# A planned attention and Fourier kernel: three quarters of the allowance for late transfers, a transfer rate three per cent higher

## The chip, the core and the metric

The kernel runs on one core of a Trainium2 chip. The metric is the device time of one execution in microseconds. Three runs of the kernel before took 2845.42, 2845.14 and 2843.12 us, so the median is 2845.14 us. The engines are PE (matrix products), ACT (exponentials and copies), DVE and POOL (elementwise work and reductions) and SP, which here only issues DMA transfers. Each engine works through its own list of instructions in order.

## The reference

Two independent blocks are computed in float32 and set side by side: a 32-head attention over 2048 positions of width 1024, and the real part of a two-dimensional Fourier transform, written as matrix products.

```python
B, S, D = 1, 2048, 1024          # H = 32 heads of Dh = 32
qkv = (x @ wqkv).reshape(B, S, 3, H, Dh)            # -> q, k, v by head
scores = einsum("bhqd,bhkd->bhqk", q, k) * Dh ** -0.5
a = einsum("bhqk,bhkd->bhqd", softmax(scores), v)   # -> (B, S, D) @ wo
u = einsum("bsd,ed->bse", xB, dft_hid_re);  w = einsum("bsd,ed->bse", xB, dft_hid_im)
b = einsum("ts,bse->bte", dft_seq_re, u) - einsum("ts,bse->bte", dft_seq_im, w)
out = concatenate([a @ wo, b], axis=-1)             # (1, 2048, 2048)
```

## The kernel before

The dense products (the projections to q, k and v, the Fourier products and the output projection) are done by a fast matrix scheme with seven products in place of eight, for the Fourier part nested twice. Each float32 operand is split into a rounded high part and the remaining low part, and each product is made of three matmuls: high by high, low by high and high by low. One such matmul is a **fill** (line 436, tiles `slot` and `hl`): 128 rows by 512 columns. The program has 6528 of them. Their operands come from DRAM: SP loads a block (`raw`, `g`, `er`, `c`, `slot`), DVE or POOL adds or subtracts two blocks (lines 501, 1312, 1354), ACT or DVE makes the high part (lines 521 and 523), POOL or DVE makes the low part (line 526). Partial sums are taken from PSUM by DVE, and stored to DRAM and read again where they don't fit in SBUF.

Attention runs head by head beside the fills. For each head PE makes scores twice: as `psS` (line 1875, letter S in the code), of which DVE takes the row maximum (line 1881) and ACT the exponential with its sum (line 1884), to get the softmax's scale; and as `psT` (line 1997, letter T), transposed and with the maximum already subtracted, of which ACT makes the exponential into `pt` (line 2001). The products of `pt` with the values (line 2016, letter V) come in runs of 20 or 24 instructions. `psS` and `psT` have two buffers each, so PE can be only two score blocks ahead of ACT.

Nothing here is ordered by the chip alone. A planner in the kernel (class `Plan`) lists every operation with its engine, a cost, what it must wait for and a rank, plays the program through in time on the host, and writes each engine's instructions down in the order in which they begin in that play. On the chip only this order is left: each instruction still waits for its true inputs. An engine whose next instruction waits for a late input stands still, with all that is listed behind it.

The planner's picture of a transfer has four numbers. Transfers follow one another at `KB_US` KiB per microsecond; a transfer lands `LANDING` (1.6 us) after its bytes; up to eight are under way; and a consumer may be placed only after the landing plus `SLACK`, an allowance by the pair of engines. `Plan.after` adds it:

```python
return d.end + (self.LAT_PE if e == "PE" else self.LAT) + self.SLACK.get((e, o.engine), 0.0)
```

The pairs are SP to POOL, SP to DVE and SP to PE; there is no pair SP to ACT. The main loop gives PE its next instruction: an attention matmul when its inputs and buffers are ready and attention is behind its share, otherwise the next fill of a fixed list, and attention again where that fill's inputs are not ready.

Of the kernel before, what the change touches and what calls it, by code (L numbers as in the profile page):

```python
# [62 lines left out]
class Plan:  # L63
# [5 lines left out]
    LAT_PE = 0.2  # L69
    OVERLAP = {"ACT": 0.13, "DVE": 0.08, "POOL": 0.08}  # L70

    SLACK = {("SP", "POOL"): 2.0, ("SP", "DVE"): 2.0, ("SP", "PE"): 2.0, ("POOL", "DVE"): 0.7}
    KB_US = 335.0
    WIDE = 0.875
    LANDING = 1.6
    QUEUE = 1.0
# [45 lines left out]
    def after(self, d, e, o):  # L122
        return d.end + (self.LAT_PE if e == "PE" else self.LAT) + self.SLACK.get((e, o.engine), 0.0)

# [7 lines left out]
    def start(self, o, e=None):  # L132
# [11 lines left out]
        if o.kb:  # L144
            for _ in range(o.lanes):
                t = max(self.free[e], self.lane[0])
                self.dma = max(self.dma, t) + o.kb / o.lanes / self.KB_US * (self.WIDE if o.wide else 1.0)
                o.end = self.dma + self.LANDING
# [2039 lines left out]
```

## Time and profile before

| what | value |
|---|---|
| median of three runs | 2845.14 us |
| profiled execution, its own time | 2845.67 us |
| its span, first to last instruction | 2843.9 us |
| outside the span | 1.8 us |
| PE busy | 2800.9 us, 98% |
| ACT busy, DVE busy | 2368.0 us and 2362.7 us, 83% each |
| POOL busy | 1212.9 us, 43% |
| moved by DMA | 768.18 MB, mean 270 GB/s |

A row of waits names the waiting instruction, an arrow, who ended the wait, and then the sum in microseconds, how many there were and the longest. A row of windows gives a stretch of the span, its length, each engine's busy time in it with the number of its instructions, the granted clock, the share of time in which the DMA engines were busy, and the bytes per second. A row of the timeline gives the start, the length and the instruction, with the idle time ahead of it in square brackets. The length of a matmul is that of the pipeline; the pace is read from one start to the next.

### The profile page before, as it was taken

To read this page: it belongs to the slowest core of one execution; us is meant where nothing else is said; L and a number is where in the kernel's file an instruction comes from. 1 tells how busy PE (TensorE), PEld (TensorE's weight loads), DVE (VectorE), ACT (ScalarE), POOL (GpSimd) and SP (SyncE) were. 2 spreads that over 40 slices of the span, in tenths; PEclk is the share of its full clock that TensorE was granted. 3 is DMA by queue.
4 is the path that set the end of the run, shared out by engine and by line. 5 is a ranking of instruction groups with operands and counts; after the bars stand their busy time and mean duration, and the time that the engine had idled before them with its cause. 6 is when DMAs were issued, how large, how long until landed. Compare 5 with 4: busy or idle time off the path is not lost.

```text
span 2843.9 us, 47011 instructions
## 1 busy us (share of the span) xinstructions
PE 2800.9 (98%) x14728; PEld 2104.3 (74%) x14728; DVE 2362.7 (83%) x3265; ACT 2368.0 (83%) x4509; POOL 1212.9 (43%) x961
## 2 busy tenths in 40 slices
PE   9999999999999999999999999999999999999999
PEld 8787776777777777777676777777677777777777
DVE  7668888778888888799888999888888898888844
ACT  5348898878988998889898898899998898898861
POOL 1235544232334443356454445666764542243300
PEclk9999999999999999999999999999999999999999
DMA  9989979699799999877899766889957675677648
GB/s 348 342 299 331 319 254 307 211 334 327 263 318 322 335 310 334 264 237 246 294 337 337 248 208 217 296 288 280 298 171 222 219 223 172 212 236 245 188 132 280
DMA packets 485845, 768.18 MB, mean 270 GB/s; under 512 B 120383, under 2 KB 153407, under 8 KB 485471
## 3 DMA queue, kind: packets, MB, share of 16 engines
q1 hardware_dynamic: 485452, 765.04, 81.4%
q8 instruction: 119, 1.95, 0.3%
q14 instruction: 130, 1.06, 0.1%
q10 hardware_dynamic: 144, 0.13, 0.0%
HBM read 511.74 MB, written 253.25 MB: 269 GB/s over the span
## 4 chain that ended last, share of the span: by engine, by line
PE 83%; DMA 7%; ACT 6%; DVE 2%; issue 1%; SPq 1%; POOL 0%; DVEq 0%; POOLq 0%; ACTq 0%
PE pd L436 37%; PE pd L2016 14%; PE psT L1997 14%; PE psS L1875 13%; PE psT L436 4%; ACT psS L1884 3%; ACT pt L2001 2%; DVE negm L1881 1%; DMA slot<-in_ct 1%; DMA tb_d<-slot 1%; DMA si_d<-slot 1%; DMA qs<-qk_d 1%; DMA ks<-qk_d 1%; DMA m_d<-lt 1%; DMA qs<-m_d 0%
## 5 line engine op out<-in xcount | busy, mean ns | idle before, releaser
L436 PE MATMUL pd<-slot,hl 128*128 128x512 f32 x5112 | 1417.1, 379 | 4.4 <-ACT hl L521 2.3
L2001 ACT ACTIVATE pt<-psT 128x512 f32<-128x512 f32 x2048 | 1209.4, 683 | 226.7 <-PE psT L1997 225.1
L1881 DVE TENSOR_REDUCE negm<-psS 128x1 f32<-128x1024 f32 x1024 | 1240.4, 1219 | 149.8 <-PE psS L1875 134.1
L1884 ACT ACTIVATE psS<-psS,negm 128x1024 f32<-128x1024 f32 x1024 | 1215.5, 1187 | 56.4 <-DVE negm L1881 55.4
L436 PEld LDWEIGHTS pd<-slot,hl 128*128 128x128 f32 x5112 | 965.7, 189 | 137.8 <-ACT hl L521 2.7
L1997 PE MATMUL psT<-qs,ks 128*128 128x512 f32 x2048 | 784.4, 386 | 2.8 <-DMA qs<-m_d 1.3
L1997 PEld LDWEIGHTS psT<-qs,ks 128*128 128x128 f32 x2048 | 383.7, 188 | 155.6 <-issue 46.9
L1875 PE MATMUL psS<-ks,qs 128*128 128x512 f32 x1552 | 458.2, 381 | 12.0 <-ACT psS L1884 11.8
L2016 PE MATMUL pd<-pt,vt 128*32 128x512 f32 x4096 | 463.7, 599 | 2.9 <-DVE c L695 1.8
L526 POOL TENSOR_TENSOR slot<-raw,slot 128x512 fp32r<-128x512 f32 x159 | 202.0, 1277 | 326.9 <-ACT slot L521 104.8
L1875 PEld LDWEIGHTS psS<-ks,qs 128*128 128x128 f32 x1552 | 286.2, 189 | 67.9 <-ACT psS L1884 24.0
L2016 PEld LDWEIGHTS pd<-pt,vt 128*32 128x32 f32 x4096 | 124.2, 110 | 286.3 <-issue 268.4
L526 POOL TENSOR_TENSOR slot<-slot,slot 128x512 fp32r<-128x512 f32 x193 | 244.6, 1279 | 203.6 <-DVE slot L523 44.5
L1884 ACT ACTIVATION_READ_ACCUMULATOR psS<-psS,negm 128x1 f32 x1024 | 314.5, 307 | 0.0
L526 POOL TENSOR_TENSOR hl<-raw,hl 128x512 fp32r<-128x512 f32 x127 | 161.8, 1276 | 228.4 <-DVE hl L523 66.2
L501 POOL TENSOR_TENSOR raw<-raw,g 128x512 f32<-128x512 f32 x126 | 161.9, 1290 | 218.8 <-DVE hl L523 28.4
L436 PE MATMUL pd<-slot,slot 128*128 128x512 f32 x780 | 201.6, 379 | 0.4 <-DVE e L745 0.4
L436 PEld LDWEIGHTS pd<-slot,slot 128*128 128x128 f32 x780 | 147.3, 189 | 21.4 <-DVE e L745 0.9
L1875 PE MATMUL psS<-ks,qx 128*128 128x512 f32 x496 | 148.2, 389 | 10.9 <-ACT psS L1884 8.9
L1875 PEld LDWEIGHTS psS<-ks,qx 128*128 128x128 f32 x496 | 90.5, 190 | 40.0 <-ACT psS L1884 15.0
L501 DVE TENSOR_TENSOR raw<-raw,g 128x512 f32<-128x512 f32 x134 | 100.0, 755 | 15.6 <-DMA g<-g_d 4.4
L2029 DVE TENSOR_TENSOR ot<-ot,pd 128x512 f32<-128x512 f32 x64 | 43.9, 685 | 70.9 <-PE pd L2016 70.1
(140 smaller groups left out, 2121.5 us busy)
## 6 DMA issues: line engine op xcount, KB each, us to landing
hl<-ha_d SPq DMA_DIRECT2D x134, 512.0 KB
slot<-in_ct SPq DMA_DIRECT2D x144, 256.0 KB
qk_d<-e SPq DMA_DIRECT2D x52, 512.0 KB
qs<-qk_d SPq DMA_DIRECT2D x128, 192.0 KB
ks<-qk_d SPq DMA_DIRECT2D x128, 192.0 KB
raw<-g_d SPq DMA_DIRECT2D x96, 256.0 KB
ha_d<-hl SPq DMA_DIRECT2D x42, 512.0 KB
raw<-in_ct SPq DMA_DIRECT2D x80, 256.0 KB
```

What stands on the lines that cost most here:

```text
L436: nc.tensor.matmul(box["ps"], a[1]((a[0].hi, a[0].lo)[u]()), turns((b[0].hi, b[0].lo)[v]()), start=k == 0, stop=k == n - 1)
L501: (nc.gpsimd if e == "POOL" else nc.vector).tensor_tensor(out=dest(), in0=dest() if a is None else a.get(), in1=other["q"] if "q" in other ...
L526: (nc.gpsimd if e == "POOL" else nc.vector).tensor_tensor(out=lo(), in0=raw(), in1=f(hi()), op=ALU.subtract)
L1875: nc.tensor.matmul(p[:, i * NB : i * NB + NB], (QX[0] if own else QS[h % 2])[:, qt * P : qt * P + P], turns(KS[h % 2][:, c * 1024 + i * NB ...
L1881: nc.vector.tensor_reduce(out=ST["negm"][:, c, qt : qt + 1], in_=box["p"], axis=AX.X, op=ALU.max, negate=True)
L1884: nc.scalar.activation(box["p"], box["p"], AF.Exp, bias=ST["negm"][:, c, qt : qt + 1], accum_out=ST["sums"][:, c, qt : qt + 1])
L1997: nc.tensor.matmul(box["p"], KS[h % 2][:, t * P : t * P + P], turns(QS[h % 2][:, j * NB : j * NB + NB]), start=True, stop=True)
L2001: nc.scalar.activation(box["t"], box["p"], AF.Exp)
L2016: nc.tensor.matmul(po["p"][j * DH : j * DH + DH, :], VT[h][:, k, :], box["t"], start=(k == t0), stop=(k == t), tile_position=(0, j * DH),)
L2029: nc.vector.tensor_tensor(out=as_two(po["o"]), in0=as_two(po["o"]), in1=order_of(po["p"]), op=ALU.add)
```

## The change

Three entries of `SLACK` go from 2.0 to 1.5 us, and `KB_US` goes from 335 to 345 KiB per microsecond. No operation is added or removed; the planner plays the same work with transfers that take less time and consumers that may follow 0.5 us earlier.

```diff
-    SLACK = {("SP", "POOL"): 2.0, ("SP", "DVE"): 2.0, ("SP", "PE"): 2.0, ("POOL", "DVE"): 0.7}
-    KB_US = 335.0
+    SLACK = {("SP", "POOL"): 1.5, ("SP", "DVE"): 1.5, ("SP", "PE"): 1.5, ("POOL", "DVE"): 0.7}
+    KB_US = 345.0
```

The order of all engines changes almost from the start. The number of matmuls of each kind stays the same. Nineteen elementwise instructions leave DVE: ten more stand on POOL (959 for 949), nine more on ACT. Counted over PE's order, 135 of the score pairs `psS` had no fill between them and the next pair, and now 138; with two fills or fewer it was 196, and now 193. When the last head's attention ends, 264 fills were left, and now 290.

PE, where the third head ends, around the 1512th fill, before. An S row with x2 is one score block; `qx` is a copy of a part of q, `pd` the PSUM tile that fills and V share:

```order
L436 MATMUL pd<-slot_5302,slot_5505 128x512 x3
L436 MATMUL pd<-slot_5347,slot_5615 128x512 x3
L1875 MATMUL psS<-ks_710,qx 128x512 x2
L1997 MATMUL psT<-qs_2707,ks_2708 128x512 x2
L1875 MATMUL psS<-ks_710,qx 128x512 x2
L1997 MATMUL psT<-qs_2707,ks_2708 128x512
L1875 MATMUL psS<-ks_710,qx 128x512 x4
L2016 MATMUL pd<-pt,vt 32x512 x24
L1875 MATMUL psS<-ks_710,qs_709 128x512 x4
L436 MATMUL pd<-slot_5183,slot_5478 128x512 x2
```

The same fills now:

```order
L436 MATMUL pd<-slot_5300,slot_5626 128x512 x3
L436 MATMUL pd<-slot_5305,slot_5639 128x512
L1875 MATMUL psS<-ks_710,qs_709 128x512 x2
L1997 MATMUL psT<-qs_2723,ks_2724 128x512
L436 MATMUL pd<-slot_5305,slot_5639 128x512 x2
L1997 MATMUL psT<-qs_2723,ks_2724 128x512
L436 MATMUL pd<-slot_5290,slot_5542 128x512 x3
L436 MATMUL pd<-slot_5295,slot_5573 128x512
L1875 MATMUL psS<-ks_710,qs_709 128x512 x2
```

The stretch of six score blocks without a fill is gone; two fills or more stand between blocks.

PE, where the fourteenth head ends, around the 3312th fill, before:

```order
L436 MATMUL pd<-slot_15720,hl 128x512 x3
L1875 MATMUL psS<-ks_2708,qx 128x512 x2
L1997 MATMUL psT<-qs_2707,ks_2708 128x512 x2
L1875 MATMUL psS<-ks_2708,qx 128x512 x2
L1997 MATMUL psT<-qs_2707,ks_2708 128x512
L1875 MATMUL psS<-ks_2708,qx 128x512 x2
L2016 MATMUL pd<-pt,vt 32x512 x24
L1997 MATMUL psT<-qs_709,ks_710 128x512 x2
L1875 MATMUL psS<-ks_2708,qx 128x512 x4
L436 MATMUL pd<-slot_15710,hl 128x512
```

The same place now. Three equal pairs of a score block and two T stand ahead of the first row, right behind the 3312th fill:

```order
L1875 MATMUL psS<-ks_2724,qs_2723 128x512 x2
L1997 MATMUL psT<-qs_709,ks_710 128x512 x2
L436 MATMUL pd<-slot_15978,hl 128x512
L1875 MATMUL psS<-ks_2724,qs_2723 128x512 x2
L1997 MATMUL psT<-qs_709,ks_710 128x512 x2
L1875 MATMUL psS<-ks_2724,qs_2723 128x512 x2
L436 MATMUL pd<-slot_15978,hl 128x512
```

Between the 3312th fill and the next there were five score blocks and five T; now there are four and eight with no V to part them, and two more blocks follow after one fill.

DVE, at the start of the program, before. The tile `er` is a block just loaded, line 526 makes a low part, line 523 a high part, line 811 takes a result from PSUM:

```order
L526 TENSOR_TENSOR slot_895<-er,slot_895 128x512
L526 TENSOR_TENSOR slot_904<-er,slot_904 128x512
L526 TENSOR_TENSOR slot_912<-er,slot_912 128x512
L523 CAST slot_941<-er 128x512
L526 TENSOR_TENSOR slot_930<-er,slot_930 128x512
L526 TENSOR_TENSOR slot_941<-er,slot_941 128x512
```

And now:

```order
L526 TENSOR_TENSOR slot_893<-er,slot_893 128x512
L523 CAST slot_921<-er 128x512
L526 TENSOR_TENSOR slot_901<-er,slot_901 128x512
L811 TENSOR_SCALAR acc_937<-pd 128x512
L526 TENSOR_TENSOR slot_921<-er,slot_921 128x512
L526 TENSOR_TENSOR slot_932<-er,slot_932 128x512
```

The high part of a later block, which waits only for a landing, now stands ahead of the low part of an earlier one.

## Prediction

> **What bounds the kernel now.** I read the page's first part, then who PE waits for, then stretches in which the transfers are at their limit, then the waits of DVE and ACT on transfers, and last single places of the timeline.
>
> ```profile
> span 2843.9 us, 47011 instructions
> PE 2800.9 (98%) x14728; PEld 2104.3 (74%) x14728; DVE 2362.7 (83%) x3265; ACT 2368.0 (83%) x4509; POOL 1212.9 (43%) x961
> ...
> PE 83%; DMA 7%; ACT 6%; DVE 2%; issue 1%; SPq 1%; POOL 0%; DVEq 0%; POOLq 0%; ACTq 0%
> ```
>
> PE is the bound: busy in 2800.9 of 2843.9 us, and 83% of the chain that ended last. All that any order can change is the other 43.0 us, and whatever new idle time it adds. Busy time flatters a pipelined engine, so here is its pace where nothing disturbs it, after the last head:
>
> ```profile
> 2797.40 2.75 PE L436 MATMUL psT<-slot,slot 128*128 128x512 f32 x12
> 2799.99 2.75 PE L436 MATMUL pd<-slot,slot 128*128 128x512 f32 x12
> ```
>
> Twelve fills begin in 2.59 us, 0.216 us each. The number of matmuls is unchanged, so PE's work is too. A place where fills don't begin at that pace is a loss.
>
> Who ends PE's waits:
>
> ```profile
> PE psS L1875 <- ACT psS L1884: 20.7, 30, 2.5
> PE pd L436 <- ACT hl L521: 2.3, 1, 2.3
> PE psS L1875 <- DMA ks<-qk_d: 1.9, 1, 1.9
> ```
>
> About half of the idle time is PE waiting for a score buffer that ACT has not emptied. That happens where no fills stand between score blocks: ACT takes longer for a block than PE. Two such places, which the order before and after shows:
>
> ```profile
> 486.58 0.48 PE L1997 MATMUL psT<-qs,ks 128*128 128x512 f32 x1
> 489.52 2.35 PE L1875 MATMUL psS<-ks,qx 128*128 128x512 f32 x4 [2.46 <-ACT psS L1884]
> 492.65 2.79 PE L2016 MATMUL pd<-pt,vt 128*32 128x512 f32 x12 [0.78 <-DVE e L745]
> ...
> 1360.92 0.70 PE L1875 MATMUL psS<-ks,qx 128*128 128x512 f32 x2 [0.61 <-ACT psS L1884]
> ...
> 1362.99 1.22 PE L1875 MATMUL psS<-ks,qx 128*128 128x512 f32 x2 [1.10 <-ACT psS L1884]
> ```
>
> The first is the end of the third head (1512th fill): 3.24 us lost. The second is the end of the fourteenth (3312th fill): 1.71 us. The planner left the fills out there because it held their inputs to be not yet there. So the planner's view of transfers decides where PE idles, and this is where the change works.
>
> **The rate.** 335 KiB per us is 335 x 1.024 = 343.0 GB/s; 345 is 353.3. What the chip moves when its DMA engines are nearly always busy:
>
> ```profile
> 40.00:80.00 40.00, 40.00 (x187) 35.04 (x186) 29.14 (x39) 17.46 (x29) 11.50 (x9) 1.00 0.99 352
> 900.00:940.00 40.00, 40.00 (x205) 31.38 (x204) 35.68 (x45) 38.40 (x75) 16.50 (x13) 1.00 1.02 356
> 1400.00:1440.00 40.00, 40.00 (x205) 31.99 (x204) 36.11 (x49) 38.19 (x75) 19.78 (x17) 1.00 0.96 344
> 1440.00:1480.00 40.00, 37.68 (x210) 24.89 (x210) 35.64 (x54) 34.58 (x68) 22.52 (x18) 1.00 1.01 345
> 1480.00:1520.00 40.00, 38.77 (x193) 28.72 (x193) 35.46 (x50) 39.34 (x78) 26.40 (x21) 1.00 0.99 345
> ```
>
> The last two columns are the busy share and the GB/s. Saturated stretches run between 344 and 356. The old rate lies just under all of them, so a planned transfer was on time or early; the new one lies inside the band. From 1400 to 1520 us the chip gives 345: the plan runs ahead by (353.3 - 345) / 345 = 2.4%, that is 2.9 us at the end of 120 us, more than the 1.5 us of allowance left. PE idles in the later two of these rows by 40.00 - 37.68 = 2.32 and 1.23 us. There the bytes limit; a plan that lists fills earlier doesn't bring them earlier, it makes PE stand at the fill and not at the score block.
>
> **The allowance.** Waits of DVE and ACT on transfers, the first and last row each (DVE has 26 rows with 42 waits, 51.1 us; ACT 14 rows with 26 waits, 40.3 us), and the longest of DVE:
>
> ```profile
> DVE slot L1354 <- DMA slot<-in_ct: 5.7, 4, 2.7
> ...
> DVE c L1070 <- DMA c<-yo_d: 0.2, 1, 0.2
> ```
>
> ```profile
> ACT slot L521 <- DMA raw<-o_d: 10.7, 5, 5.3
> ...
> ACT hl L521 <- DMA raw<-in_wqk: 0.3, 1, 0.3
> ```
>
> ```profile
> 498.62 0.69 DVE L837 TENSOR_TENSOR c<-e,c 128x512 f32<-128x512 f32 x1 [4.30 <-DMA c<-u_d]
> ```
>
> Even with 2.0 us allowed, DVE stood 42 times at a transfer that came late, once for 4.30 us. Behind a standing DVE are the row maxima (line 1881), behind those the exponentials on ACT, behind those PE's score buffers.
>
> **The sum**, against the profiled execution's 2845.67 us, which is 0.53 above the median.
>
> 1. Fills between score blocks. Lost at the end of the third head: 3.24 us, which the new order removes. At the end of the fourteenth it has four score blocks and eight T in a row, with no V between them, where it had five blocks, five T and a V; the loss of 1.71 us there grows. Over the whole order the count of score pairs without a fill goes from 135 to 138, of those with at most two from 196 to 193. I take 0. The ends: all 20.7 us of the wait on ACT gone, or as much again.
> 2. Allowance. Each of DVE's 42 waits may get 0.5 us longer: 21.0 us of DVE. What reaches PE: at most PE's whole idle time over DVE's and ACT's late-transfer waits, 43.0 / (51.1 + 40.3) = 0.47, so 9.9 us; at least 0, where the buffers cover it. ACT has no entry in the allowance, and its waits move only with the rate. POOL also follows 0.5 us sooner, but with 43% busy it has time to wait. Waits that are new are not in the 21.0. I take 6, nearer the upper end because DVE is 83% busy.
> 3. Rate. Four saturated stretches (the start, around 620, around 920, and 1400 to 1520 us), each at most 2.9 us behind the plan: 11.6 us at most, 0 where the plan doesn't fill the queue. The rows at 352 and 356 leave little, those at 344 and 345 the whole: 2 us.
> 4. Nineteen instructions leave DVE. By the rows below ten of 0.73 and nine of 0.47 us make 12 us off DVE in the whole span; ACT and POOL take them beside other work. 0, hidden by PE's 98%. The 26 fills that now come after the last head only move within a fixed sum: 0, since PE has no gap there.
>
> ```profile
> L526 DVE TENSOR_TENSOR slot<-raw,slot 128x512 fp32r<-128x512 f32 x95 | 68.4, 734 | 10.1 <-ACT slot L521 9.5
> L523 DVE CAST hl<-raw 128x512 fp32r<-128x512 f32 x159 | 73.7, 466 | 8.1 <-PE pd L436 7.5
> ```
>
> Together +8: 2853.7 on the profiled execution, 2853 as a median, 0.3% slower. A change of less than 0.2% (5.7 us) can't be told from none.
>
> **The rivals.**
>
> *Fewer stretches without fills: faster.* If the plan's old allowance was what kept the fills back, not the bytes, its removal brings PE work where it idled. For it: the third head's loss is gone in the new order, and from 900 to 940 us PE is full (40.00) while the DMA engines are too, so a saturated queue alone doesn't stop it. Against it: the counts 135 and 138. If half of the 20.7 us goes, and no wait is added: 2835. It decides if DVE's late-transfer waits stay under about 55 us. The Trainium skill, "DMA: Bandwidth & Descriptors", section Specifications, gives about 358 GB/s as one core's share of the memory; by that the plan's 353.3 would still be a rate that the chip can keep, term 3 would be 0, and this rival likelier. The rows at 344 and 345 with a busy share of 0.99 and more don't reach that figure; those at 352 and 356 nearly do.
>
> *No measurable change.* PE's 43.0 us are so few, and the places where it idles so scattered (the longest single wait is 2.5 us), that gains and losses of terms 1 to 3 cancel: 2840 to 2851. For it: the same counts; against it: almost every row of the order is new, and nothing holds the sum of some hundred small waits to within 5 us.
>
> *Much slower.* One long stand of PE at a fill whose block is late, with attention listed behind it, at each saturated stretch: term 3's 11.6 and term 2's 9.9 us in full, 2867.
>
> **How the numbers follow.** Slower, with 2853 as its likeliest and 2867 as its far end: 0.57. No measurable change: 0.21. Faster, around 2835: 0.22. The range 2833 to 2868 leaves out the lower part of the faster case and a little beyond the far end, some 2 in 10.
>
> **What would show it.** DVE's and ACT's waits on transfers together rise from 91 to about 110 us, DVE's share of that most. PE's waits for operands that ACT, DVE or POOL made late (lines 521, 523, 526), of which the longest row above has 2.3 us, grow by several us, and PE's busy share of the span falls. The gap at the end of the third head is gone, that at the end of the fourteenth is longer. From 1400 to 1520 us the DMA rate stays at about 345 GB/s. I am wrong if late-transfer waits don't grow, or grow on engines that nobody waits for, or if PE's wait on ACT at line 1875 moves by more than 10 us either way, which would make term 1 the one that decides.

## The result and the profile after

Ten runs of each kernel: 2851.91 us median after (2846.02 to 2854.88), 2846.69 before (2841.79 to 2851.15). The ratio is 1.0019, with a 95% interval from 1.0011 to 1.0028: the changed kernel is slower by 0.19%, or 5.2 us by the medians. The forecast was 2853 us within 2833 to 2868, and slower as the likeliest case; a change under 5.7 us, it said, could not be told from none, but with ten runs of each kernel 5.2 us could. The profiled execution took 2854.24 us against 2845.67.

The first part of the page of after, its busy times and its chain:

```profile
span 2852.4 us, 47045 instructions
PE 2802.0 (98%) x14728; PEld 2100.6 (74%) x14728; DVE 2367.5 (83%) x3246; ACT 2372.5 (83%) x4518; POOL 1224.6 (43%) x971
...
PE 78%; DMA 8%; ACT 6%; DVE 4%; issue 2%; SPq 1%; POOL 1%; DVEq 0%; POOLq 0%; ACTq 0%
```

The span grew by 8.5 us. PE's busy time grew by 1.1, and its idle time from 43.0 to 2852.4 - 2802.0 = 50.4 us: nearly all of the growth is PE standing. Busy time is not pure work, though. The profiled execution of before had 17.1 us at half clock inside the kernel and that of after 6.8 (last section), which alone should have taken some 5 us off PE's busy time; this is an estimate, half of the difference. So about 6 us of busy time were lost elsewhere, and the groups by line don't show where. By line, from the groups of PE (busy time, mean ns, then the idle time just before them and who ended it), first before, then after:

```profile
L1997 PE MATMUL psT<-qs,ks 128*128 128x512 f32 x2048 | 784.4, 386 | 2.8 <-DMA qs<-m_d 1.3 <-ACT pt L2001 1.1
L2016 PE MATMUL pd<-pt,vt 128*32 128x512 f32 x4096 | 463.7, 599 | 2.9 <-DVE c L695 1.8 <-DVE e L745 0.8 <-DVE c L693 0.4
L1875 PE MATMUL psS<-ks,qs 128*128 128x512 f32 x1552 | 458.2, 381 | 12.0 <-ACT psS L1884 11.8
...
L1875 PE MATMUL psS<-ks,qx 128*128 128x512 f32 x496 | 148.2, 389 | 10.9 <-ACT psS L1884 8.9 <-DMA ks<-qk_d 1.9
```

```profile
L1997 PE MATMUL psT<-qs,ks 128*128 128x512 f32 x2048 | 787.3, 388 | 7.3 <-DMA qs<-m_d 4.9 <-ACT pt L2001 2.0 <-DMA tg_d<-raw 0.2
L1875 PE MATMUL psS<-ks,qs 128*128 128x512 f32 x1552 | 460.0, 383 | 20.1 <-ACT psS L1884 19.7
L2016 PE MATMUL pd<-pt,vt 128*32 128x512 f32 x4096 | 459.3, 594 | 6.1 <-DVE c L693 1.9 <-DVE c L695 1.2 <-DVE slot L693 0.9
...
L1875 PE MATMUL psS<-ks,qx 128*128 128x512 f32 x496 | 145.9, 386 | 3.5 <-ACT psS L1884 3.5
```

The score blocks (both forms of line 1875) lose 22.9 us before and 23.6 after (20.1, and 3.5 of the form with `qx`): little. T at line 1997 loses 4.5 us more, 3.6 of them on the transfer `qs<-m_d`; V at line 2016 loses 3.2 more, behind DVE. The fills (line 436) lose 1.8 less.

The new wait is the row maxima of a head, on their way from DVE over DRAM (`m_d`) into the rows of `qs` that subtract them (line 1923). Its longest place, in PE's timeline of after (idle time in brackets):

```profile
1120.03 1.22 PE L1997 MATMUL psT<-qs,ks 128*128 128x512 f32 x2 [3.26 <-DMA qs<-m_d]
```

SP had issued that transfer at 1116.17 us, so PE stood through most of its flight: T was listed before its data could be there.

Waits of DVE and ACT on transfers, after, the first and last row of DVE and then of ACT:

```profile
DVE raw L501 <- DMA raw<-in_wd: 7.9, 4, 2.1
...
DVE slot L1354 <- DMA qs<-qk_d: 0.3, 1, 0.3
```

```profile
ACT slot L521 <- DMA raw<-o_d: 8.8, 4, 4.8
...
ACT hl L521 <- DMA er<-in_wqk: 0.5, 1, 0.5
```

DVE has 31 rows with 58 waits and 66.5 us (before 42 waits, 51.1 us). ACT has 10 rows with 19 waits and 30.9 us (before 26 and 40.3). Together 91.4 became 97.4 us. POOL's waits on transfers went from 353.7 to 379.0 us, but PE waited for POOL only 0.6 us in either kernel.

The two gaps that the order showed, as windows of before and then of after (length, busy time of PE, PEld, DVE, ACT and POOL, granted clock, DMA share, GB/s):

```profile
480.00:500.00 20.00, 16.25 (x81) 7.59 (x80) 13.39 (x20) 11.72 (x21) 5.00 (x4) 0.83 0.86 280
1355.00:1375.00 20.00, 18.29 (x97) 10.23 (x95) 17.18 (x30) 15.20 (x30) 8.83 (x7) 0.91 0.61 187
```

```profile
480.00:500.00 20.00, 20.00 (x101) 16.34 (x94) 16.21 (x19) 17.42 (x34) 6.60 (x6) 1.00 0.98 309
1360.00:1380.00 20.00, 16.11 (x58) 10.43 (x57) 15.92 (x18) 18.14 (x36) 13.92 (x12) 0.91 0.89 267
```

At the end of the third head PE idled 3.75 us and now not at all. At the end of the fourteenth it idled 1.71 us and now 3.89.

### The profile page after: what moved, and what is told of

It reads as the page before. It is cut to its first block, busy times and chain, and to the rows that moved or that the text cites. A ratio compares the mean times of both kernels' runs of the same rounds, so it can differ in the third digit from the quotient of the medians.

```text
span 2852.4 us, 47045 instructions
## 1 busy us (share of the span) xinstructions
PE 2802.0 (98%) x14728; PEld 2100.6 (74%) x14728; DVE 2367.5 (83%) x3246; ACT 2372.5 (83%) x4518; POOL 1224.6 (43%) x971
## 3 DMA queue, kind: packets, MB, share of 16 engines
q8 instruction: 119, 1.95, 0.3%
## 4 chain that ended last, share of the span: by engine, by line
PE 78%; DMA 8%; ACT 6%; DVE 4%; issue 2%; SPq 1%; POOL 1%; DVEq 0%; POOLq 0%; ACTq 0%
PE pd L436 35%; PE pd L2016 13%; PE psT L1997 13%; PE psS L1875 12%; PE psT L436 4%; ACT psS L1884 4%; ACT pt L2001 2%; DVE negm L1881 2%; DMA g<-in_ct 1%; DMA qs<-m_d 1%; DMA slot<-in_ct 1%; DMA raw<-in_wd 1%; DMA slot<-so_d 1%; DMA m_d<-lt 0%; DMA qs<-qk_d 0%
## 5 line engine op out<-in xcount | busy, mean ns | idle before, releaser
L1875 PE MATMUL psS<-ks,qs 128*128 128x512 f32 x1552 | 460.0, 383 | 20.1 <-ACT psS L1884 19.7
L526 POOL TENSOR_TENSOR slot<-slot,slot 128x512 fp32r<-128x512 f32 x207 | 262.4, 1282 | 181.0 <-DVE slot L523 33.3
L501 POOL TENSOR_TENSOR raw<-raw,g 128x512 f32<-128x512 f32 x120 | 153.9, 1289 | 236.3 <-DMA g<-g_d 14.6
L436 PEld LDWEIGHTS pd<-slot,slot 128*128 128x128 f32 x780 | 147.4, 189 | 20.5
L1875 PEld LDWEIGHTS psS<-ks,qx 128*128 128x128 f32 x496 | 90.5, 190 | 29.2 <-ACT psS L1884 8.2
```

What stands on the lines that cost most here:

```text
L436: nc.tensor.matmul(box["ps"], a[1]((a[0].hi, a[0].lo)[u]()), turns((b[0].hi, b[0].lo)[v]()), start=k == 0, stop=k == n - 1)
L501: (nc.gpsimd if e == "POOL" else nc.vector).tensor_tensor(out=dest(), in0=dest() if a is None else a.get(), in1=other["q"] if "q" in other ...
L526: (nc.gpsimd if e == "POOL" else nc.vector).tensor_tensor(out=lo(), in0=raw(), in1=f(hi()), op=ALU.subtract)
L1875: nc.tensor.matmul(p[:, i * NB : i * NB + NB], (QX[0] if own else QS[h % 2])[:, qt * P : qt * P + P], turns(KS[h % 2][:, c * 1024 + i * NB ...
```

## The experiments

The theory to test is the prediction's: a smaller allowance makes transfers come late, DVE stands, and PE behind it; the rate adds a little. Its rivals: that the rate, or the pair SP to PE alone (the wait `qs<-m_d`), carries the loss; and that the number itself hardly matters, because any other order of some 14,700 matmuls leaves PE some microseconds more or less (scatter). Each edit is shown against the kernel before, and each ratio is to runs of the kernel before in the same series.

### The two halves, and two steps too small to matter

```diff
-    SLACK = {("SP", "POOL"): 2.0, ("SP", "DVE"): 2.0, ("SP", "PE"): 2.0, ("POOL", "DVE"): 0.7}
+    SLACK = {("SP", "POOL"): 1.5, ("SP", "DVE"): 1.5, ("SP", "PE"): 1.5, ("POOL", "DVE"): 0.7}
```

> Only the allowance changes, 2.0 to 1.5 us, at the old rate of 335. Late-transfer theory (consumers are listed ahead of data that comes late): most of the 0.19% is here, ratio 1.001 to 1.002, DVE's waits on transfers rise from 51 us to 60 or more. Reshuffle theory (any edit of the planner's numbers gives another order, and its time is drawn anew within some tenths of a per cent): a ratio anywhere from 0.998 to 1.004, not tied to DVE's waits on transfers.

Measured: 1.0037 [1.0023, 1.0050], 2853.99 us. The allowance alone costs at least as much as both edits. But that is more than the prediction's theory expected of it (1.001 to 1.002), DVE's waits on transfers are 46.4 us in 41 waits, shorter than before, and T's wait for `qs<-m_d` is 1.3 us, as before. The sign agrees with the prediction's theory, the mechanism doesn't.

```diff
-    KB_US = 335.0
+    KB_US = 345.0
```

> Only the rate changes, 335 to 345, at the old allowance of 2.0 us. Late-transfer theory: 1.0005 to 1.001, since only the stretches in which the DMA engines are full get later than planned; this and the allowance alone add up to about 1.0019. Reshuffle theory: anywhere from 0.998 to 1.004, and the two parts don't add up.

Measured: 0.9988 [0.9979, 0.9996], 2840.70 us. The rate alone makes the kernel a little faster, with 40.4 us of DVE waits. The prediction's theory had a small loss here. The parts multiply to 1.0037 x 0.9988 = 1.0025, inside the interval of the whole change. That they add up was not what scatter leads one to expect, but it decides little: by the intervals of the parts the product may be anything from 1.000 to 1.005.

```diff
-    KB_US = 335.0
+    KB_US = 336.0
```

> The rate goes from 335 to 336, 0.3%: a planned transfer of 256 KiB takes 2 ns less. Late-transfer theory: nothing that can be measured, ratio 0.9995 to 1.0005. Reshuffle theory: the order is another one all the same, and the ratio may be as far from 1 as that of the whole change, by 0.001 to 0.004 either way.

Measured: 0.9987 [0.9978, 0.9995], 2838.81 us, and DVE's waits fell to 28.3 us. A tenth of the rate step gives the same gain as the whole step.

```diff
-    SLACK = {("SP", "POOL"): 2.0, ("SP", "DVE"): 2.0, ("SP", "PE"): 2.0, ("POOL", "DVE"): 0.7}
+    SLACK = {("SP", "POOL"): 1.95, ("SP", "DVE"): 1.95, ("SP", "PE"): 1.95, ("POOL", "DVE"): 0.7}
```

> The allowance goes from 2.0 to 1.95 us. Late-transfer theory: a tenth of the allowance's part, under 0.0003, so nothing that can be measured. Reshuffle theory: as far from 1 as the whole change, by 0.001 to 0.004 either way.

Measured: 1.0033 [1.0021, 1.0045], 2851.75 us. A tenth of the allowance step costs as much as the whole step, with fewer late transfers (41.1 us in 34 waits) and no wait of note for `qs<-m_d` (0.8 us). The allowance differs by only 0.05 us in this plan, but nearly the whole of PE's order differs with it. PE's wait for score buffers with the rate of 336, and then with the allowance of 1.95:

```profile
PE psS L1875 <- ACT psS L1884: 17.7, 34, 0.7
```

```profile
PE psS L1875 <- ACT psS L1884: 23.1, 47, 1.3
```

The smallest steps in the two numbers give results of either sign, and neither interval reaches 1. That speaks for scatter.

### A control, and far steps

```diff
-    LANDING = 1.6
+    LANDING = 1.601
```

> The planned landing is 1 ns later (1.601 us), and only a few dozen rows of the orders differ from those of the kernel before. A control: both theories expect 0.9995 to 1.0005. If it is 0.001 off or more, then not even the order is what moves the time, but the spread from run to run.

Measured: 1.0000 [0.9991, 1.0009], 2843.82 us. Only a few dozen rows of PE's order differ here, and the time is that of before. So the losses of 0.3 to 0.4% above come from other orders, not from building or measuring a second time. For the gains of 0.1% that is less sure: their intervals overlap the control's.

```diff
-    SLACK = {("SP", "POOL"): 2.0, ("SP", "DVE"): 2.0, ("SP", "PE"): 2.0, ("POOL", "DVE"): 0.7}
+    SLACK = {("SP", "POOL"): 0.0, ("SP", "DVE"): 0.0, ("SP", "PE"): 0.0, ("POOL", "DVE"): 0.7}
```

> No allowance at all (0 in place of 2.0 us) at the old rate. Late-transfer theory: four times the step of the change; DVE's waits on transfers go well over 80 us and the time to 1.008 or more. Reshuffle theory: one more draw, 0.998 to 1.004, with DVE's waits on transfers saying little about the time.

Measured: 1.0174 [1.0158, 1.0189], 2895.30 us. Now the trend shows: DVE's waits on transfers double to 101.4 us in 88 waits, and PE stands at T:

```profile
PE psS L1875 <- ACT psS L1884: 25.0, 39, 2.4
PE psT L1997 <- DMA qs<-m_d: 20.0, 13, 4.4
```

```diff
-    SLACK = {("SP", "POOL"): 2.0, ("SP", "DVE"): 2.0, ("SP", "PE"): 2.0, ("POOL", "DVE"): 0.7}
+    SLACK = {("SP", "POOL"): 3.0, ("SP", "DVE"): 3.0, ("SP", "PE"): 3.0, ("POOL", "DVE"): 0.7}
```

> An allowance of 3.0 us at the old rate. Late-transfer theory: DVE's waits on transfers fall below 35 us and the kernel is a little faster, 0.997 to 1.000, unless the fills come too late. Reshuffle theory: one more draw, 0.998 to 1.004.

Measured: 1.0029 [1.0018, 1.0041], 2852.18 us, with only 32.6 us of DVE waits and none for `qs<-m_d`. Half as much allowance again makes the late transfers fewer and the kernel slower, by as much as a cut of 0.05 us. Fewer late transfers alone buy nothing near the old setting.

```diff
-    KB_US = 335.0
+    KB_US = 375.0
```

> A rate of 375 KiB per us (384 GB/s, above all that the trace of the kernel before shows) at the old allowance. Late-transfer theory: the plan runs ahead of the chip by some 11% in saturated stretches, waits on transfers grow, 1.004 or more. Reshuffle theory: 0.998 to 1.004, and the time follows how long PE waits for ACT at the score blocks, whichever way that falls.

Measured: 1.0147 [1.0134, 1.0160], 2885.52 us; DVE's waits 98.6 us in 86, T's wait for `qs<-m_d` 15.6 us. 375 KiB/us is 384 GB/s, above every 40 us stretch seen here. So the rate does have a price when it is too high. A quarter of this step (345) in proportion would have been +0.37%; it measured -0.12%.

### Which pair of engines

```diff
-    SLACK = {("SP", "POOL"): 2.0, ("SP", "DVE"): 2.0, ("SP", "PE"): 2.0, ("POOL", "DVE"): 0.7}
+    SLACK = {("SP", "POOL"): 2.0, ("SP", "DVE"): 2.0, ("SP", "PE"): 0.0, ("POOL", "DVE"): 0.7}
```

> The allowance of the pair SP to PE alone goes to 0, the pairs SP to POOL and SP to DVE keep 2.0 us, rate 335. PE theory (the damage of a short allowance is PE itself standing at the start of a head for the row maxima that come back from DRAM, the transfer qs<-m_d): most of what 0 for all pairs costs is here, 1.006 or more, PE's waits on qs<-m_d near the 20 us of that run. DVE theory (POOL and DVE standing at late blocks is what counts, as the prediction had it): 0.998 to 1.004 here, and the loss in the run with 0 for POOL and DVE.

Measured: 1.0071 [1.0056, 1.0086], 2867.75 us. DVE's waits fell to 32.2 us; PE's waits at T carry the loss:

```profile
PE psS L1875 <- ACT psS L1884: 20.8, 39, 1.1
PE psT L1997 <- DMA qs<-m_d: 20.1, 14, 4.5
```

The wait at T is 18.8 us above before's 1.3, and the medians differ by 22.0 us. The two agree only roughly, and partly by chance: PE's idle time grew by 14.1 us in all (43.0 to 57.1), because its other waits became shorter, and the other 8.6 us of the span's growth are PE busy time (2800.9 to 2809.5 us).

```diff
-    SLACK = {("SP", "POOL"): 2.0, ("SP", "DVE"): 2.0, ("SP", "PE"): 2.0, ("POOL", "DVE"): 0.7}
+    SLACK = {("SP", "POOL"): 0.0, ("SP", "DVE"): 0.0, ("SP", "PE"): 2.0, ("POOL", "DVE"): 0.7}
```

> The pairs SP to POOL and SP to DVE go to 0, SP to PE keeps 2.0 us, rate 335. DVE theory: 1.010 or more, DVE's waits on transfers near 100 us. PE theory: DVE's waits on transfers rise as much, to 80 us or more, but little of it reaches PE: 1.004 to 1.008, and PE's waits on qs<-m_d stay under 3 us.

Measured: 1.0198 [1.0179, 1.0217], 2901.95 us. Here `qs<-m_d` costs PE nothing and DVE pays. DVE's first and last row on transfers (44 rows, 96 waits, 122.1 us), then ACT's wait for the row maxima (55.4 us before), and then PE's waits:

```profile
DVE slot L501 <- DMA slot<-in_ct: 15.7, 7, 5.3
...
DVE e L1113 <- DMA slot<-so_d: 0.3, 1, 0.3
```

```profile
ACT psS L1884 <- DVE negm L1881: 86.4, 89, 9.7
```

```profile
PE psS L1875 <- ACT psS L1884: 38.7, 50, 3.9
PE psT L1997 <- ACT pt L2001: 6.2, 8, 1.2
PE pd L436 <- ACT hl L521: 5.3, 1, 5.3
```

DVE and ACT wait 122.1 + 46.0 - 91.4 = 76.7 us longer for transfers than before, and the span is 56.0 us longer (2899.9 against 2843.9): 0.73 us for each. Of the 56.0, 31.9 are PE idle time, 0.42 for each, and 24.1 are PE busy time; the granted clock, 0.994 against 0.996, explains some 6 of the latter (two thousandths of the span, an estimate). The reading that the pair SP to PE alone carries the loss falls (it asked for at most 1.008 here). The prediction's chain is there, late transfer, DVE, ACT's exponentials, PE's score buffers, once the step is large. POOL's allowance was changed together with DVE's, so the run doesn't part the two. With all three pairs at 0 the loss is no larger (1.0174), so the two effects don't add.

### The change with one part undone

```diff
-    SLACK = {("SP", "POOL"): 2.0, ("SP", "DVE"): 2.0, ("SP", "PE"): 2.0, ("POOL", "DVE"): 0.7}
-    KB_US = 335.0
+    SLACK = {("SP", "POOL"): 1.5, ("SP", "DVE"): 1.5, ("SP", "PE"): 2.0, ("POOL", "DVE"): 0.7}
+    KB_US = 345.0
```

> The changed kernel with one part undone: the pair SP to PE back at 2.0 us, POOL and DVE at 1.5, rate 345. PE theory: PE's waits on qs<-m_d fall from 4.9 us to under 3, and the ratio goes from 1.0019 towards 1.000, as far as the spread between neighbouring orders (0.001 to 0.004) lets it be seen. DVE theory: 1.002.

Measured: 1.0038 [1.0024, 1.0052], 2856.03 us. T's wait for `qs<-m_d` shrank from 4.9 us in the changed kernel to 1.9, but the time grew: DVE's waits are 77.3 us, and in the profiled execution, 6.1 us above the median, the score blocks wait longer:

```profile
PE psS L1875 <- ACT psS L1884: 29.2, 32, 5.4
PE psT L1997 <- DMA qs<-m_d: 1.9, 3, 0.7
```

```diff
-    SLACK = {("SP", "POOL"): 2.0, ("SP", "DVE"): 2.0, ("SP", "PE"): 2.0, ("POOL", "DVE"): 0.7}
-    KB_US = 335.0
+    SLACK = {("SP", "POOL"): 2.0, ("SP", "DVE"): 2.0, ("SP", "PE"): 3.0, ("POOL", "DVE"): 0.7}
+    KB_US = 345.0
```

> The rate of 345 with POOL and DVE at 2.0 us and SP to PE at 3.0 us. The run with the rate alone had 0.9988 with 3.7 us of PE waits on qs<-m_d. PE theory: these go to under 1 us and the time with them, 0.996 to 0.999. If only the spread between orders counts: 0.998 to 1.004.

Measured: 1.0001 [0.9990, 1.0012], 2846.20 us. The wait at T is gone (0.3 us) and no gain came of it; PE's wait for score buffers is 29.6 us instead of 19.8 with the rate of 345 alone, but this profiled execution took 6.8 us more than the median of its kernel, and the other 0.2, so part of that may be the execution and not the order.

### What the series says together

The ratios are of all runs. The waits and PE's idle time (span less PE's busy time) are of one execution each, which lay between 3.3 us under and 6.8 us over the median of its kernel.

| allowance POOL, DVE, PE (us) | rate (KiB/us) | ratio | DVE late, us | T late, us | PE on score buffers, us | PE idle, us |
|---|---|---|---|---|---|---|
| 2.0, 2.0, 2.0 | 335 (before) | 1 | 51.1 | 1.3 | 20.7 | 43.0 |
| 2.0, 2.0, 2.0, landing 1.601 | 335 (control) | 1.0000 | 49.6 | 0.2 | 20.5 | 40.6 |
| 1.5, 1.5, 1.5 | 345 (after) | 1.0019 | 66.5 | 4.9 | 23.2 | 50.4 |
| 1.5, 1.5, 1.5 | 335 | 1.0037 | 46.4 | 1.3 | 22.8 | 50.0 |
| 1.95, 1.95, 1.95 | 335 | 1.0033 | 41.1 | 0.8 | 23.1 | 43.5 |
| 3.0, 3.0, 3.0 | 335 | 1.0029 | 32.6 | 0 | 23.2 | 41.6 |
| 2.0, 2.0, 2.0 | 336 | 0.9987 | 28.3 | 0.4 | 17.7 | 35.9 |
| 2.0, 2.0, 2.0 | 345 | 0.9988 | 40.4 | 3.7 | 19.8 | 37.6 |
| 2.0, 2.0, 3.0 | 345 | 1.0001 | 47.9 | 0.3 | 29.6 | 46.1 |
| 1.5, 1.5, 2.0 | 345 | 1.0038 | 77.3 | 1.9 | 29.2 | 51.0 |
| 2.0, 2.0, 0 | 335 | 1.0071 | 32.2 | 20.1 | 20.8 | 57.1 |
| 2.0, 2.0, 2.0 | 375 | 1.0147 | 98.6 | 15.6 | 29.9 | 73.1 |
| 0, 0, 0 | 335 | 1.0174 | 101.4 | 20.0 | 25.0 | 75.1 |
| 0, 0, 2.0 | 335 | 1.0198 | 122.1 | 0.5 | 38.7 | 74.9 |

Two things are laid over each other. There is a trend: the four far steps into too little allowance or too high a rate cost 0.7 to 2.0%, and late transfers show where. And there is scatter: five settings near the old one or on its safe side (allowances from 1.95 us up, rates 335 to 345, without the control) lie between 0.9987 and 1.0033, in no order of the numbers. The change's 1.0019 lies inside that scatter. Two settings, the rates 336 and 345 with the old allowance, are 0.1% faster than the kernel before; by the same reading they are lucky orders, not better estimates of the rate.

The last column sorts better than the times do. The three orders with 1.5 us for POOL and DVE have 50.0 to 51.0 us of PE idle time (mean 50.5); the seven with 1.95 us or more for all pairs at rates up to 345, before and control among them, have 35.9 to 46.1 (mean 41.2); the far steps have 57.1 and more. No run was made to test this, and the figures are of one execution each, but it speaks for a price of the allowance of several microseconds that the scatter of the whole times hides. With the allowances of 3.0 and 1.95 us, for one, the loss is not idle time: PE's busy time is 4.7 and 3.4 us above before's.

## Why the prediction was right, and where it wasn't

The number and the sign came out: the steps summed to +8 us, and the two profiled executions differ by 8.6, the medians by 5.2. Much of that is luck. The five settings of the scatter alone, put on the 2845 us of before, give 2841 to 2855 us, all inside the stated range, so that landing in it says little for the mechanism. How the steps fared:

- **Term 1, fills between score blocks, 0.** Right, in both details: the third head's gap is gone, the fourteenth's is longer (3.89 us for 1.71), and PE's idle time at line 1875 moved by 0.7 us. The counts 135 and 138 were no guide to more than that.
- **Term 2, allowance, +6.** Right in part for the changed kernel: DVE's waits rose by 15.4 us of the 21.0 that were the upper end. ACT's fell by 9.4, so that both together came to 97 us, not 110. The next link of the prediction's chain, ACT waiting for the row maxima of a late DVE, did not grow but shrank. Before, and then after:

```profile
ACT psS L1884 <- DVE negm L1881: 55.4, 64, 9.3
```

```profile
ACT psS L1884 <- DVE negm L1881: 48.4, 59, 4.3
```

  What the prediction said would show it on PE, longer waits for operands of ACT, DVE and POOL (lines 521, 523, 526), didn't happen: these sum to 4.5 us after and 5.9 before. The loss showed at T (+4.5 us) and V (+3.2 us) instead. V's two longest waits for DVE, 1.91 us up to 632.82 and 1.24 us up to 713.14 us, are no late transfers either: in the 13 us ahead of each DVE waited for no transfer, but had other work listed first. Only behind the third, 0.90 us up to 345.80, stands a wait of DVE on a transfer (1.25 us). As a cause of these 5 us the step isn't shown: with the allowance alone cut, the kernel lost 0.37% while DVE waited less than before. PE's idle time, higher in all three orders with 1.5 us, speaks for some price of the allowance, but by which waits it comes is open. The factor of at most 0.47 held for PE's idle time where the step was large (0.42), not for the whole time (0.73).
- **Term 3, rate, +2.** Wrong in its ceiling. The sum took 345 GB/s as what the chip gives from 1400 to 1520 us. The same windows after, behind the one from 900 us:

```profile
900.00:940.00 40.00, 39.28 (x219) 27.93 (x218) 35.23 (x45) 35.62 (x68) 17.68 (x14) 1.00 1.02 373
1400.00:1440.00 40.00, 38.97 (x207) 28.45 (x211) 36.46 (x52) 37.31 (x73) 23.70 (x19) 1.00 0.97 354
1440.00:1480.00 40.00, 37.55 (x209) 26.01 (x202) 33.50 (x43) 34.16 (x66) 17.78 (x15) 1.00 1.01 353
1480.00:1520.00 40.00, 39.62 (x211) 30.18 (x213) 36.45 (x56) 39.71 (x80) 24.29 (x20) 1.00 0.99 354
```

  They give 353 and 354, just the rate that the new plan asks for, and from 900 us even 373. That the old plan's windows gave 345 was no limit; why the same 40 us move more in one order than in another, no run here separates. The comparison also left out the factor `WIDE`: the planner gives the 208 blocks of 512 KiB that lines 1263, 1368 and 1607 move, a seventh of all bytes, only 0.875 of the time. For these the old plan asked for 335 x 1.024 / 0.875 = 392 GB/s and the new one for 404, both above every stretch seen here, so the old rate was not under all of them. The rate alone measured -0.12%.
- **Term 4, work that leaves DVE, 0.** Nothing speaks against it: DVE's busy time even rose by 4.8 us with 19 instructions fewer.
- **What the steps left out.** The pair SP to PE was named in the change and priced nowhere. It has a wait of its own, T behind `qs<-m_d`, which made 3.6 of the 7.4 us of new idle time, and 18.8 us where it alone was cut to 0. The place could have been found beforehand: before's groups show it at line 1997 with 1.3 us, in a chain of two transfers in a row.
- **What any order can change.** The prediction took this to be PE's 43.0 us of idle time and what is added to them, with PE's busy time fixed. In the runs the busy time went from 2800.1 to 2825.0 us for the same matmuls, so a part of each loss lies where no wait shows it.
- **The rival "no measurable change"** is just missed: its range ended at 2851 us, and 2851.91 was measured. The argument that the prediction raised against it, that almost every row of the order is new and nothing holds the sum of some hundred small waits within 5 us, is what the series shows at this size. But scatter has no direction, and so it is no reason for slower either.

What stays open is which differences between the two orders make the 5.2 us, and how much of it is the allowance's own price. In the times no part of the change, alone or undone, gives a consistent price; in PE's idle time the allowance does, by figures read afterwards.

## What to carry to other kernels

When a planner writes the whole order of a full engine, a small step in one of its constants is a draw among orders: measure it beside a neighbouring step, a step far out and a control that leaves the order nearly as it was, before giving its result a cause. Here neighbours differ by up to 0.46%, and in the times only steps of several times the change's size showed the constant's own price. Split each difference into idle and busy time of the bounding engine: the first may sort where the time doesn't. Cost each pair of an allowance by itself: the one in front of the bounding engine has a wait of its own there (18.8 us more, where the time grew by 22.0), the others reach it through buffers (76.7 us more of waits, 31.9 more of PE idle time).

## What the hardware showed that was not expected

**Half clock after short stands of PE.** The granted clock of before falls to about a half in stretches inside the kernel, each behind one or two of PE's stands. Three windows: two on such stretches of before, then one of after.

```profile
489.00:496.00 7.00, 5.70 (x20) 1.79 (x24) 3.85 (x5) 4.98 (x10) 1.27 (x1) 0.51 0.94 304
1363.00:1366.20 3.20, 3.20 (x14) 1.08 (x18) 2.92 (x8) 2.79 (x6) 1.27 (x1) 0.50 0.86 249
```

```profile
1372.40:1375.70 3.30, 3.30 (x7) 2.20 (x8) 2.30 (x3) 3.30 (x7) 1.61 (x2) 0.50 0.96 240
```

The stretches last 3.41 us or twice that: at 127.3, 489.1 (6.83 us), 574.5 and 1362.9 us before, at 1119.7 and 1372.3 after. So a stand can cost more than its own length. It need not: a stand of 2.33 us that ended at 118.39 us of before brought no such stretch, and the granted clock was 1.00 from 115 to 122 us. The same run of 48 V matmuls behind the stand of 2.46 us at 489.52, and undisturbed, in the timeline of before:

```profile
492.65 6.97 PE L2016 MATMUL pd<-pt,vt 128*32 128x512 f32 x48 [0.78 <-DVE e L745]
...
2775.17 5.36 PE L2016 MATMUL pd<-pt,vt 128*32 128x512 f32 x48
```

Over 65 runs of the kernel before, a thousandth less of mean granted clock goes with 2.3 us more time (correlation -0.60). Worked out, a thousandth of 2844 us is 5.7 us at half clock, in which 2.8 us of matmuls are lost. So the half clock would account for a part of the spread of one program's runs.

It differs between orders too. The mean granted clock was 0.9970 over those 65 runs, 0.9984 over the ten of the changed kernel, 0.9989 and 0.9982 over the eleven each with the rates of 345 and 336 alone. At 2.3 us for each thousandth, which is an estimate, this is worth 3 us to the changed kernel, whose order then loses some 8 elsewhere, and 4 and 3 us to the other two, whose medians gained 2.9 and 4.8. Their gain is thus about what their fuller clock gives.

The Trainium skill, "TensorE: Matmul & The Clock Gate", Part 1, tells of a free-running window of 3413 ns and a return to half rate after an idle window. The length agrees with the stretches of 3.41 us. The page's section "Why this matters for your kernels" asks for no gap over about 3 us; here less was enough: ahead of 1362.9 us in the kernel before, PE had stood 0.61 and 1.10 us only.

**A saturated rate is not one number.** Stretches of 40 us with the DMA engines busy for 0.97 or more ran at anything from 321 to 373 GB/s over all these runs. The Trainium skill, "DMA: Bandwidth & Descriptors", Bandwidth, gives each of two streaming cores about 358 GB/s and calls its higher figures those of one core alone. One core runs here, and 373 agrees with that: the 358 against which the prediction weighed the new rate was no ceiling for it.
